# The first unit's third d_ff step in plain blocks: a fused attention and star-ReLU MLP kernel

## Chip, cores and metric

The kernel runs on 1 core of one Trainium2 chip. The metric is the device time of one execution in microseconds; the median of 4 runs of the kernel before is 912.08 us (910.40 to 912.98).

## The reference

Linear attention per head, with a root-mean-square norm, then an MLP on the 4608 tokens (8 batches x 576) of 512 features:

```python
kv = np.einsum('bhsd,bhse->bhde', k, v)
out = np.einsum('bhsd,bhde->bhse', q, kv)
x = out / np.sqrt(np.mean(out * out, axis=-1, keepdims=True) + 1e-06) * g_norm
...
h = x @ w_in            # 512 -> 2048
r = np.maximum(h, 0.0)
g = s * (r * r) + b
return g @ w_out        # 2048 -> 512
```

All is float32 but the two weight matrices, which arrive with 64 bits an element; the kernel makes float32 of them itself.

## The kernel before, in words

**Units and stages.** The tokens are worked in nine units of 512. A unit has a first stage (x @ w_in, and the activation) and a second stage (g @ w_out). The attention of the next unit is laid between the matmuls. The order of instructions on each engine is the order in which the program's Python calls them: the schedule is written out by hand, and an engine takes its instructions in that order.

**First stage.** The 2048 columns of w_in are four steps s = 0 to 3 of 512 columns. A step can be computed in two ways.
- In plain blocks (`mm1_plain`, L671): four blocks of 256 columns x 256 tokens over all 512 features, each 8 matmuls 128x128 by 256. In the order a11, a12, a21, a22 they alternate between the PSUM tiles x and y (two buffers each). ACT takes the x blocks out with a ReLU and DVE squares them (L691); DVE takes the y blocks out with a clamp (L686) and squares them.
- By a scheme of seven products (`mm1`, L707): a Strassen-Winograd step, which forms sums of quarters of w_in and of x first and then needs seven products of 4 matmuls where plain blocks need eight. They are x1, z2, x6, y7, x5, x3, y4. x1, x6, x5 and x3 add up in one PSUM tile x; after x1, x6 and x5 ACT copies the intermediate sum to SBUF (L718) before the next product may add to the tile. `sums_w_in(s)` (L264) makes the sums of w_in on DVE, in two halves: s12 (two operations, of which the second is needed by x6) and s34 (two more: the one for y7, and the one for x3). `x_sums(u)` (L601) makes the four sums of x, in two halves.

The affine pass s * g + b of the activation runs on ACT (L644). In unit 0 it is put off: finished squares go on a list, and `scale_g` (L667) empties it.

**Weights in unit 0.** Sixteen blocks of weights (0 to 7 w_in, two to a step; 8 to 11 the upper half of w_out, `w_up`; 12 to 15 the lower, `w_dn`) are loaded by the SP queue into three buffers `w_raw` (`load_w`, L185). Each is converted in four operations: `raw(i)` is two on ACT (L225, L230), `convert(i)` two on DVE (L235, L245). When a block's conversion is done, the load three blocks ahead is sent (`plus`, L1510). `more(i)` makes a difference of w_out quarters on DVE, in w_up itself.

**The order around the change.** In unit 0, steps 0 and 1 run in plain blocks (the list `slots0`, eight slots, L1536), steps 2 and 3 by the scheme. `first_unit` (L1633) writes the order out: the dictionary `beside` says which conversions, sums and the like are called after each slot's block, and after each slot comes scale_g. Then the products of step 2 (a) and step 3 (b) follow in one list, mixed with conversions 8 to 12. The last two products of step 3, x3 and y4, come after the first product of the second stage (L1786 on), and conversions 13 to 15 lie in the second stage's first slots. There the SP queue also stores sums of w_out to DRAM for the later units (`store_w2`, L315), loads K and V of batch 1 and the q of unit 1.

**Unit 1** runs all four steps by the scheme, so that the sums of w_in that unit 0 did not need must be made there: sums_w_in(0) late in unit 0's second stage, and in `sides` (L1685) sums_w_in(1) at point 1 of step 0 (after z2). Points 2 and 3 follow x6 and y7.

Of the kernel before, what the change touches and what calls it, by code (L numbers as in the profile page):

```python
# [16 lines left out]
def kernel(  # L17
# [53 lines left out]
    NS = FC // 4  # L71
# [192 lines left out]
    def sums_w_in(s):  # L264
        ws[s] = wp.tile([P, 3, KH, 2, P], FP32, name=f"ws_{s}")
        a11, a12 = wa[s][:, :KH], wa[s][:, KH:]
        a21, a22 = wb[s][:, :KH], wb[s][:, KH:]
        s1, s2, s4 = (ws[s][:, i] for i in range(3))

        def s12():  # L270
            add(s1, a21, a22)
            sub(s2, s1, a11)

        def s34():
            sub(a21, a11, a21)
            sub(s4, a12, s2)

        return s12, s34
# [383 lines left out]
    def g_s1(s):  # L662
        add(ga["s1", s], ga["a21", s], ga["a22", s])
# [3 lines left out]
    def scale_g():  # L667
        while to_scale:
            affine(to_scale.pop(0))
# [863 lines left out]
    gp = ctx.enter_context(tc.tile_pool(name="gp", bufs=NS // 2))  # L1533


    slots0 = [slot for s in range(2) for slot in mm1_plain(s)]  # L1536
    turn[0]()
    turn[1]()
    take[0]()
# [85 lines left out]
    def raw(i):  # L1625
        hi(i)
        lo(i)

    def convert(i):
        shift(i)  # L1630
        plus(i)

    def first_unit():  # L1633
        sums = {}

        def of_w(s, k):
            if k == 0:
                sums[s] = sums_w_in(s)
            sums[s][k]()

        of_x = x_sums(0)
        beside = {
            1: [partial(raw, 3), partial(convert, 3)],
            2: [partial(raw, 4), partial(convert, 4)],
            3: [partial(raw, 5), partial(convert, 5)],
            4: [partial(raw, 6), partial(of_w, 2, 0), of_x[0]],
            5: [partial(raw, 7), partial(of_w, 2, 1), partial(g_s1, 0)],
            6: [partial(raw, 8), of_x[1], partial(convert, 6)],
            7: [partial(convert, 7)],
        }  # L1650
        for n, slot in enumerate(slots0):
            if n > 1:
                out_of = slot()
                if out_of:
                    out_of()
            for fn in beside.get(n, []):
                fn()
            scale_g()
        a, b = (mm1(0, s) for s in (2, 3))
        for fn in (  # L1660
            a["x1"], partial(g_s1, 1), partial(of_w, 3, 0),
            a["z2"],
            a["x6"], partial(of_w, 3, 1), partial(raw, 9), scale_g,
            a["y7"], partial(convert, 8),
            a["x5"], partial(raw, 10),
            b["x1"], partial(convert, 9), scale_g,
            a["x3"], partial(more, 8),
            b["z2"], partial(raw, 11),
            a["y4"], a["y4_square"], partial(convert, 10),
            b["x6"], a["x3_s1"], scale_g,  # L1670
            b["y7"], partial(convert, 11),
            b["x5"], partial(raw, 12), partial(more, 9), partial(more, 10), partial(more, 11),
            partial(convert, 12), scale_g,
        ):
            fn()
        return b

    def x3(a):
        a["x3"]()
# [5 lines left out]
    def sides(u, A, B):  # L1685

        first, second = {}, {}
        kv = []  # L1690
        if u in kv_due:
            kv.append(lambda: kv_product(kv_due[u], u > 2))
            kv.append(lambda: used(*((u, "kv", (n, m)) for n in range(NP) for m in range(2))))
        q = {half: [partial(loads, u + 2, half)] for half in range(2)}
        if u == 1:
            first[0, 1] = list(sums_w_in(1))
            first.update({
                (1, 3): kv,
                (2, 0): [partial(A["turn"], 0), partial(A["turn"], 1)],
                (2, 1): [A["product"]],  # L1700
                (2, 2): [A["back"]],
                (2, 3): [A["square"]],
                (3, 0): [A["row_sum"]],
                (3, 2): [A["norm"], A["turn_x"]],
                (3, 3): [lambda: [load() for load in load_q(12, rest_on=nc.sync)]],
            })
            return first, second
        if u + 1 == U:
            return first, second
        if u == 2:  # L1710
            first = {
                4: [A["turn"]],
                5: kv,
                8: [A["product"]],
                9: [A["back"], B["turn"]],
                10: [A["square"]],
                11: [A["row_sum"]],
                12: [B["product"]],
                13: [A["norm"]],
                14: [A["turn_x"]],  # L1720
                15: [B["back"], *q[0]],
            }
            second = {
                0: [B["square"]], 1: [B["row_sum"], A["scale"]], 2: [B["norm"]], 3: [B["turn_x"], *q[1]],
                "sums": [B["scale"]],
            }
        else:
            first = {
                2: [A["turn"]],
                4: [A["product"], *kv],  # L1730
                5: [A["back"]],
                6: [A["square"], B["turn"]],
                7: [A["row_sum"]],
                8: [A["norm"]],
                9: [A["turn_x"]],
                10: [B["product"], *q[0]],
                11: [B["back"], A["scale"]],
                12: [B["square"]],
                13: [B["row_sum"]],
                14: [B["norm"]],  # L1740
                15: [B["turn_x"], *q[1]],
            }
            second = {1: [B["scale"]]}
        second[5], second[6] = [[lambda n=n: x_sums(u + 1)[n]()] for n in range(2)]
        return first, second

    for u in range(U):
        A, B = pairs_of(u + 1) if u + 1 < U else (None, None)
        if u == 0:
            last = first_unit()  # L1750
            second = mm2(0)
        else:
            if u == 1:
                loads(2, 0)
                loads(2, 1)
            first, at_second = sides(u, A, B)
            if u > 1:
                run, last = mm1_deep(u)
                second = mm2(u, last, at_second)
                run(lambda n: [fn() for fn in first.get(n, [])], second["early"])  # L1760
                second["rest"]()
                continue
            steps = [mm1(u, s) for s in range(NS)]
            second = mm2(u)
        for s in range(NS if u > 0 else 0):
            a = steps[s]

            def at(n):
                for fn in first.get((s, n), []):
                    fn()  # L1770

            at(0)
            a["x1"]()
            if s:
                x3(steps[s - 1])
            a["z2"]()
            at(1)
            if s:
                y4(steps[s - 1])
            a["x6"]()  # L1780
            at(2)
            a["y7"]()
            at(3)
            a["x5"]()
        side = side_of(A, B, lambda: [fn() for fn in x_sums(u + 1)], u)
        for n, slot in enumerate(second):  # L1786
            slot()
            if u == 0:
                if n == 0:
                    store_w2(1, 5)  # L1790
                    for name in ("x3", "y4", "y4_square"):
                        last[name]()
                    raw(13)
                    scale_g()
                    convert(13)
                    load_kv(1, 0, convp, tag="raw", bufs=3)
                    raw(14)
                    last["x3_s1"]()
                elif n == 1:
                    convert(14)  # L1800
                    load_kv(1, 1, convp, tag="raw", bufs=3)
                    raw(15)
                    loads(1, 0)
                    loads(1, 1)
                elif n == 2:
                    convert(15)
                    t2 = convp.tile([P, 4 * R * D], FP32, name="w_t2", tag="raw", bufs=3)
                    W2_AT[6] = t2[:, : FC // 2 * HN].rearrange("p (f n) -> p f n", n=HN)
                elif n == 4:
                    store_w2(3, 2)  # L1810
                    sub_w_out(6, 3, 5)
                    store_w2(6)
            if n == 0 and u > 0:
                x3(steps[-1])
                y4(steps[-1])
            for step in side.get(n, []):
                step()
        if u == 0:
            tc_late()
            pump()  # L1820
# [30 lines left out]
```

## Time and profile before

| What | Value |
|---|---|
| median of 4 runs (lowest to highest) | 912.08 us (910.40 to 912.98) |
| the profiled execution's own time | 911.95 us |
| its span, first to last instruction | 910.1 us, so 1.85 us lie around it |
| mean granted clock of TensorE over the span | 0.998 |
| unit 0's first stage: end of the eighth plain block, first product of step 2 | 53.03 us |
| first product of unit 0's second stage | starts 78.58 us |
| w_raw loads sent between 37 and 47 us, from issue to landing | 5.4 to 6.1 us |
| w_raw loads sent between 56 and 80 us | 4.9 to 5.1 us |

Engines are PE (matmul), PEld (its weight load), DVE, ACT, POOL and SP. A row of the timeline gives the start in us from the span's start, the length, the engine, the line of the program, the operation with the tile it writes and those it reads, the shape, how many, and in brackets how long the engine sat idle before it and who ended that. On PE one float32 matmul of 256 columns leaves two records, so x8 is a product of four matmuls and x16 a plain block of eight. Lengths of matmuls overlap with the next one; the time a group takes is read from its start to the start of the next. The chain of waits follows the last instruction of a stretch back, at each step to what released it.

### The profile page before, as it was taken

How to read it: one execution, taken by the hardware profiler on the slowest of the kernel's cores; microseconds unless marked ns; L12 is line 12 of the kernel's file. 1: busy time of each engine (PE TensorE's matmuls, PEld its weight loads, DVE VectorE, ACT ScalarE, POOL GpSimd, SP SyncE). 2: the span in 40 equal slices, each digit the busy share in tenths (PEclk: the TensorE clock that was granted, in tenths of full speed). 3: DMA queues.
4: the chain of work that ended last, by engine and by line, in shares of the span. 5: the costliest groups of instructions: out<-in, count | busy, mean ns of one | idle time of the engine just before them, and what ended most of it. 6: DMA issues, size and time to landing. Idle time of an engine off the chain costs nothing.

```text
span 910.1 us, 19226 instructions
## 1 busy us (share of the span) xinstructions
PE 896.7 (99%) x7506; PEld 824.1 (91%) x7506; DVE 667.7 (73%) x1234; ACT 359.5 (40%) x606; POOL 227.5 (25%) x432
## 2 busy tenths in 40 slices
PE   7989999999999999999999999999999999999998
PEld 6878888888889998999889998999899989999998
DVE  2898676588557985887678857895878778874686
ACT  2878224531147215640366026701580057104710
POOL 2000016113524242810273035603440300021000
PEclk9999999999999999999999999999999999999999
DMA  9657977339943894379636973597438812891286
GB/s 257 220 187 248 286 192 233 104 82 370 354 142 76 276 337 145 78 227 309 215 70 177 294 258 90 123 309 255 132 87 283 293 36 56 275 304 49 58 257 184
DMA packets 120139, 180.34 MB, mean 198 GB/s; under 512 B 29169, under 2 KB 46321, under 8 KB 120049
## 3 DMA queue, kind: packets, MB, share of 16 engines
q1 hardware_dynamic: 101552, 153.00, 54.1%
q0 software_dynamic: 15040, 23.88, 9.1%
q10 hardware_dynamic: 3456, 2.23, 1.0%
q8 instruction: 60, 0.98, 0.5%
q14 instruction: 31, 0.25, 0.1%
HBM read 153.36 MB, written 25.69 MB: 197 GB/s over the span
## 4 chain that ended last, share of the span: by engine, by line
PE 90%; DVE 5%; DMA 2%; ACT 1%; issue 1%; ACTq 0%; DVEq 0%
PE x_ps L91 47%; PE y_ps L91 26%; PE z_ps L91 9%; PE sx_ps L91 4%; PE y_ps L545 2%; DMA kv_sb<-in_v_dram 1%; PE kv_ps L366 1%; PE z_ps L366 1%; DMA w_raw<-in_moe_w_in_dram 1%; DVE xs L253 1%; DVE xn L578 0%; DVE a L253 0%; DVE wa L245 0%; DVE sub L253 0%; PE y_ps L366 0%
## 5 line engine op out<-in xcount | busy, mean ns | idle before, releaser
L1623 POOL DMA_DIRECT2D q_sb<-in_q_dram x256 | 143.6, 569 | 133.9 <-ACT a L652 63.0
L1210 POOL DMA_DIRECT2D out_dram<-o x110 | 54.8, 505 | 399.1 <-issue 152.6
L91 PE MATMUL x_ps<-w_sb,sub 128*128 128x128 f32 x1176 | 148.8, 275 | 0.6 <-DVE r L250 0.6
L91 PEld LDWEIGHTS x_ps<-w_sb,sub 128*128 128x128 f32 x1176 | 139.7, 192 | 0.9 <-DVE r L250 0.9
L91 PE MATMUL x_ps<-xs,ws 128*128 128x256 f32 x544 | 130.0, 382 | 2.9 <-ACT r L718 2.9
L91 PE MATMUL y_ps<-xs,wb 128*128 128x256 f32 x544 | 129.1, 382 | 0.0
L644 ACT ACTIVATE a<-a,b_col,s_col 128x512 f32<-128x512 f32 x144 | 116.2, 813 | 25.5 <-DVE a L647 20.9
L91 PEld LDWEIGHTS x_ps<-xs,ws 128*128 128x128 f32 x544 | 100.3, 191 | 15.9 <-ACT r L718 3.7
L91 PEld LDWEIGHTS y_ps<-xs,wb 128*128 128x128 f32 x544 | 101.4, 191 | 13.6 <-issue 0.6
L819 ACT COPY a<-x_ps 128x512 f32<-128x512 f32 x28 | 16.4, 584 | 216.0 <-PE x_ps L91 215.8
L91 PE MATMUL x_ps<-xT,wa 128*128 128x256 f32 x336 | 78.3, 381 | 0.1
L250 DVE TENSOR_TENSOR r<-sx_ps,a 128x256 f32<-128x256 f32 x63 | 26.6, 422 | 62.1 <-PE sx_ps L91 62.0
L91 PEld LDWEIGHTS x_ps<-xT,wa 128*128 128x128 f32 x336 | 62.2, 190 | 9.7 <-issue 1.5
L91 PE MATMUL x_ps<-w_sb,a 128*128 128x128 f32 (+1 forms) x432 | 64.9, 298 | 0.0
L91 PE MATMUL y_ps<-w_sb,a 128*128 128x128 f32 (+1 forms) x416 | 62.1, 295 | 0.0
L91 PEld LDWEIGHTS x_ps<-w_sb,a 128*128 128x128 f32 x432 | 58.9, 191 | 3.3 <-issue 0.4
L91 PEld LDWEIGHTS y_ps<-w_sb,a 128*128 128x128 f32 x416 | 56.1, 192 | 2.1
L250 DVE TENSOR_TENSOR a<-y_ps,r 128x512 f32<-128x512 f32 x40 | 27.6, 689 | 41.1 <-PE y_ps L91 30.8
L250 DVE TENSOR_TENSOR r<-x_ps,o 128x256 f32<-128x256 f32 (+1 forms) x84 | 29.7, 353 | 29.3 <-PE x_ps L91 28.6
L91 PE MATMUL y_ps<-w_sb,sub 128*128 128x128 f32 x392 | 49.5, 275 | 0.0
L647 DVE SCALAR_TENSOR_TENSOR a<-a 128x512 f32<-128x512 f32 x67 | 46.4, 692 | 2.3
L253 DVE TENSOR_TENSOR a<-a,a 128x512 f32<-128x512 f32 x72 | 46.8, 684 | 0.4
(185 smaller groups left out, 1513.1 us busy)
## 6 DMA issues: line engine op xcount, KB each, us to landing
w_sb<-w SPq DMA_DIRECT2D x385, 256.0 KB, 4.5
w_raw<-in_moe_w_in_dram SPq DMA_DIRECT2D x8, 1024.0 KB, 6.1
w_raw<-in_moe_w_out_dram SPq DMA_DIRECT2D x8, 1024.0 KB, 5.0
w_sb<-w SPq DMA_DIRECT2D x14, 512.0 KB, 8.9
w<-sub POOLq DMA_DIRECT2D x28, 256.0 KB, 6.4
w_sb<-in_k_dram SPq DMA_DIRECT2D x24, 288.0 KB, 5.6
w_sb<-in_v_dram SPq DMA_DIRECT2D x24, 288.0 KB, 5.7
out_dram<-o POOLq DMA_DIRECT2D x92, 64.0 KB, 4.0
```

What stands on the lines that cost most here:

```text
L91: nc.tensor.matmul(o, lhsT=lhsT, rhs=rhs, start=start, stop=stop, skip_group_check=True)
L250: nc.vector.tensor_tensor(out=o, in0=a, in1=b, op=ALU.add)
L253: nc.vector.tensor_tensor(out=o, in0=a, in1=b, op=ALU.subtract)
L366: nc.tensor.matmul(ps[r][(r ^ l) * HB : (r ^ l) * HB + HB, i, :], lhsT=kv[l][0][rows, j, :], rhs=kv[l][1][rows, j, :], start=(j == 0), sto ...
L545: nc.tensor.matmul(ps[l][32 * p : 32 * p + 32, r, lo:hi], lhsT=bd_kv[b % 2][rows, p, at : at + 32], rhs=st["qT"][rows, p, lo:hi], start=Tr ...
L644: nc.scalar.activation(t, t, AF.Identity, scale=s_col, bias=b_col)
L647: nc.vector.scalar_tensor_tensor(t, t, 0.0, t, ALU.max, ALU.mult)
L819: nc.scalar.copy(g_tile("a11", s), st["x", s])
L1210: queues[s % 2].dma_start(out=view[b, jj, :, cols], in_=st[name, j][s * w : s * w + w, cols])
L1623: load()
```

## The change

Unit 0 runs step 2 in plain blocks too: `slots0` has twelve slots, and only step 3 uses the scheme. The order around it is new. After the block of slot n (1 to 8) come raw(n + 2) and convert(n + 2), one conversion to a slot; after slot 9 come the first half of sums_w_in(3) and more(8), after slot 10 the sums of x around raw(11), after slot 11 the second half of sums_w_in(3). g_s1 comes after the blocks of slots 4 and 8, ahead of the conversions. Conversions 11 and 12 lie among the five products of step 3, with raw(13) behind them; convert(13) stays in the second stage's first slot. The sums of w_in for step 2, no longer made in unit 0, are made in unit 1's step 0 at point 3, ahead of x5.

```diff
-    slots0 = [slot for s in range(2) for slot in mm1_plain(s)]
+    slots0 = [slot for s in range(NS - 1) for slot in mm1_plain(s)]
...
     def first_unit():
...
-        beside = {
-            1: [partial(raw, 3), partial(convert, 3)],
-            2: [partial(raw, 4), partial(convert, 4)],
-            3: [partial(raw, 5), partial(convert, 5)],
-            4: [partial(raw, 6), partial(of_w, 2, 0), of_x[0]],
-            5: [partial(raw, 7), partial(of_w, 2, 1), partial(g_s1, 0)],
-            6: [partial(raw, 8), of_x[1], partial(convert, 6)],
-            7: [partial(convert, 7)],
-        }
         for n, slot in enumerate(slots0):
             if n > 1:
                 out_of = slot()
                 if out_of:
                     out_of()
-            for fn in beside.get(n, []):
-                fn()
-            scale_g()
-        a, b = (mm1(0, s) for s in (2, 3))
+                if n % 4 == 0:
+                    g_s1(n // 4 - 1)
+            if 0 < n < 9:
+                raw(n + 2)
+                convert(n + 2)
+            elif n == 0:
+                continue
+            elif n == 9:
+                of_w += sums_w_in(3)
+                of_w[0]()
+            elif n == 10:
+                of_x[0]()
+                raw(11)
+                of_x[1]()
+            else:
+                of_w[1]()
+            if n < 11:
+                scale_g()
+            if n == 9:
+                more(8)
+        a = mm1(0, NS - 1)
         for fn in (
-            a["x1"], partial(g_s1, 1), partial(of_w, 3, 0),
-            a["z2"],
-            a["x6"], partial(of_w, 3, 1), partial(raw, 9), scale_g,
-            a["y7"], partial(convert, 8),
-            a["x5"], partial(raw, 10),
-            b["x1"], partial(convert, 9), scale_g,
-            a["x3"], partial(more, 8),
-            b["z2"], partial(raw, 11),
-            a["y4"], a["y4_square"], partial(convert, 10),
-            b["x6"], a["x3_s1"], scale_g,
-            b["y7"], partial(convert, 11),
-            b["x5"], partial(raw, 12), partial(more, 9), partial(more, 10), partial(more, 11),
-            partial(convert, 12), scale_g,
+            a["x1"], scale_g, partial(convert, 11), partial(more, 9),
+            a["z2"], partial(raw, 12),
+            a["x6"], scale_g, partial(g_s1, 2),
+            a["y7"], partial(convert, 12),
+            a["x5"], partial(raw, 13), scale_g, partial(more, 10), partial(more, 11),
         ):
             fn()
...
         if u == 1:
-            first[0, 1] = list(sums_w_in(1))
+            for s in range(1, NS - 1):
+                first[((0, 1), (0, 3))[s - 1]] = list(sums_w_in(s))
...
                     for name in ("x3", "y4", "y4_square"):
                         last[name]()
-                    raw(13)
+                    convert(13)
                     scale_g()
-                    convert(13)
```

More of the change, by code (lines that the diff above doesn't have):

```diff
@@ L1633, in first_unit @@
     def first_unit():
[L1634 to L1639, printed above, removed]
-        of_x = x_sums(0)
-        beside = {
-            1: [partial(raw, 3), partial(convert, 3)],
-            2: [partial(raw, 4), partial(convert, 4)],
-            3: [partial(raw, 5), partial(convert, 5)],
-            4: [partial(raw, 6), partial(of_w, 2, 0), of_x[0]],
-            5: [partial(raw, 7), partial(of_w, 2, 1), partial(g_s1, 0)],
-            6: [partial(raw, 8), of_x[1], partial(convert, 6)],
-            7: [partial(convert, 7)],
-        }
+        of_x = x_sums(0)
+        of_w = []
         for n, slot in enumerate(slots0):
@@ L1655, in first_unit @@
                     out_of()
-            for fn in beside.get(n, []):
-                fn()
-            scale_g()
-        a, b = (mm1(0, s) for s in (2, 3))
-        for fn in (
-            a["x1"], partial(g_s1, 1), partial(of_w, 3, 0),
-            a["z2"],
-            a["x6"], partial(of_w, 3, 1), partial(raw, 9), scale_g,
-            a["y7"], partial(convert, 8),
-            a["x5"], partial(raw, 10),
-            b["x1"], partial(convert, 9), scale_g,
-            a["x3"], partial(more, 8),
-            b["z2"], partial(raw, 11),
-            a["y4"], a["y4_square"], partial(convert, 10),
-            b["x6"], a["x3_s1"], scale_g,
-            b["y7"], partial(convert, 11),
-            b["x5"], partial(raw, 12), partial(more, 9), partial(more, 10), partial(more, 11),
-            partial(convert, 12), scale_g,
+                if n % 4 == 0:
[19 more added lines that the diff above has]
+        a = mm1(0, NS - 1)
+        for fn in (
+            a["x1"], scale_g, partial(convert, 11), partial(more, 9),
[3 more added lines that the diff above has]
+            a["x5"], partial(raw, 13), scale_g, partial(more, 10), partial(more, 11),
         ):
             fn()
-        return b
+        return a
     def x3(a):
```

## The prediction

> **What bounds the kernel now.** The page first: how full each engine is.
>
> ```profile
> span 910.1 us, 19226 instructions
> ...
> PE 896.7 (99%) x7506; PEld 824.1 (91%) x7506; DVE 667.7 (73%) x1234; ACT 359.5 (40%) x606; POOL 227.5 (25%) x432
> ```
>
> PE is the bound: time is gained only by fewer PE instructions, or by taking away one of PE's rare waits. PE's waits by releaser show that the longest is a single one:
>
> ```profile
> PE x_ps L91 <- ACT r L718: 2.9, 1, 2.9
> ```
>
> The stretches around it (PE, PEld, DVE, ACT and POOL busy, granted clock, DMA share, GB/s):
>
> ```profile
> 53.00:56.50 3.50, 3.50 (x17) 2.86 (x16) 3.47 (x6) 2.81 (x3) 0.00 (x0) 1.00 0.00 0
> 56.50:59.50 3.00, 0.15 (x1) 0.00 (x0) 2.93 (x5) 1.28 (x2) 0.00 (x0) 1.00 0.40 115
> ...
> 60.43:63.85 3.42, 3.42 (x10) 2.72 (x9) 3.35 (x7) 1.37 (x2) 0.00 (x0) 0.50 1.01 338
> ```
>
> While PE stands still DVE is full, and 0.9 us after PE resumes its clock is 0.50 for 3.4 us. The timeline of PE gives the size of both, row by row (start, length):
>
> ```profile
> 53.03 1.89 PE L91 MATMUL x_ps<-xT,wa 128*128 128x256 f32 x8
> 54.76 1.89 PE L91 MATMUL z_ps<-xT,wa 128*128 128x256 f32 x8
> 59.52 2.92 PE L91 MATMUL x_ps<-xs,ws 128*128 128x256 f32 x8 [2.87 <-ACT r L718]
> 62.24 2.69 PE L91 MATMUL y_ps<-xs,wb 128*128 128x256 f32 x8
> 64.76 1.89 PE L91 MATMUL x_ps<-xs,ws 128*128 128x256 f32 x8
> ...
> 78.58 3.62 PE L91 MATMUL x_ps<-w_up,a 128*128 128x256 f32 x16
> ```
>
> The reader is to take starts, not lengths: a product of the scheme (x8 here) takes 1.73 us from start to start, a plain block (x16) 3.45 (49.58 to 53.03). The chain of waits says why x6 of the third step starts late:
>
> ```profile
> 54.95 0.61 DVE wa L235
> 55.57 0.02 issue
> 55.59 1.23 DVE wa L245
> 56.82 0.61 DVE a L686
> 57.43 0.02 issue
> 57.45 0.70 DVE a L691
> 58.16 0.03 issue
> 58.18 0.81 ACT a L644
> 59.00 0.48 ACT r L718
> ```
>
> x1 was done at 54.9, but its copy (L718) stood on ACT behind the affine pass (L644) of the last plain block, and that stood behind DVE, which did sums and a conversion (L235, L245) before it looked at the block (L686, L691). DVE's backlog is the cause.
>
> **The change on PE.** Both kernels are alike up to the end of the eighth plain block at 53.03. From there to the first product of the second stage (78.58) before has 12 products: 12 x 1.727 = 20.72 us. The stretch is 25.55, so 4.83 are lost: 2.87 of waiting, 1.19 and 0.76 in the two products at the half clock (2.92 and 2.48, by starts, against 1.73). After has four plain blocks and five products: 4 x 3.454 + 5 x 1.727 = 22.45 us. So the plain third step costs 1.73 more (13.82 against 12.09), the lost 4.83 go, and without a new wait the second stage starts at 75.48: 3.10 us gained. PE is fed without any longer wait from there on, so a shift passes through to the end.
>
> **What is late next.** I place the new order by the durations of before. On DVE an independent 128x512 operation starts 0.60 us after the last, one that needs the last 0.72 (the rows at 51.26 to 54.87 and 57.45); a conversion takes 0.72 + 1.14 = 1.86. Both kernels' DVE finishes block 5 at 46.66. Until the square of the twelfth block is done, DVE then has five conversions (9.3), four clamp-and-square pairs (5.32), three single squares (1.8), two sums s1 (1.2), two w sums (1.32), one w_out difference (0.6), four x sums (2.52), one square at the head (0.61): 22.7 us, so 69.3. Conversions in before also waited on ACT for 0.21 to 0.56 us in this stage; three at 0.3 make it 70.2. The block itself leaves PE at 66.85, so DVE is some 2 us behind, but what hangs on it has room:
> - x6 (70.31) needs the copy r1, whose ACT is free: done at 69.4. Room 0.9.
> - y7 (72.03) needs the difference in wb, next on DVE: 70.9. Room 1.1.
> - x5 (73.76) needs the copy r2 of x6. On ACT it stands behind the affine pass of the twelfth block (0.72) and raw(12), 1.05 + 1.05 with L225 and L230: 70.3 + 0.72 + 2.1 = 73.15, copy 0.58: 73.75. **Room none.** Each further 0.1 us on DVE is 0.1 us on PE here.
> - The second stage (75.5) needs w_up: converted at 73.4. Room 2.1.
>
> What can make DVE later are the loads: three w_raw buffers, and each load is sent when the conversion three blocks earlier ends. Those sent at 37.6 to 46.8 took 5.4 to 6.1 us beside each other, w_out blocks sent alone 4.9 to 5.1. Now w_out blocks are sent every 3.2 to 3.4 us, two in flight. ACT ends raw(8) at 55.0, as in before, and after one affine pass wants block 9 at 55.7; sent at 50.1, it lands at 55.3 if it takes 5.2 us. With 4.9 the wait at x5 is about 0.1, with 6.1 about 1.0. I take 5.2 to 5.4, nearest to the row at 46.75 (5.37, a w_out load beside another), and **0.3 us**. DMA has room for it: 338 to 419 GB/s in busy stretches, and 1.05 MB every 3.3 us is 318.
>
> **Other edits, at nothing.** x sums, w_out differences and g_s1 are the same operations, moved; they are in the sum above. convert(13) moves into the second stage with more room than before, since w_dn is wanted at 92.8 and the conversions end some 4 us earlier. The SP queue's stores, K/V and q loads come behind the w_raw loads; those end about 7 us earlier, PE's need only 3. The four sums of the third step move to unit 1, 4 x 0.6 = 2.4 us of DVE ahead of a22 of step 0. There DVE is idle 1.55 and then 3.16 us (147.10 and 151.68), and a22, 0.9 late, must be read by 151.4: it covers them. With that cover gone, up to 2.4.
>
> **Sum.** -4.83 + 1.73 + 0.3 = -2.8. The profiled execution took 911.95 (0.13 below the median of 912.08): 909.15, on the median 909.3. I say 909.2.
>
> **A rule against it.** The half clock is 1.95 of the 4.83 and goes only if the wait caused it. The row: 2.87 us idle, then 0.50 for 3.4 us. The Trainium skill, "TensorE: Matmul & The Clock Gate", Part 1, "What's actually happening", says the clock halves after at least one idle window of about 3.4 us, windows running free. By that rule 2.87 us isn't enough, the half clock had another cause and stays, and the sum is -0.85. The trace decides here: its half clock lasts one such stretch, directly after the only long wait.
>
> **Rivals.**
> - *Late loads* (10%): the new pace makes loads take 6.5 to 7 us; block after block reaches ACT late, x6, y7 and x5 wait 1.2 to 2.0 us in all. 911.95 - 3.10 + 1.2 to 2.0 = 910.05 to 910.85. For it: the DMA share is 1.01 in busy stretches, and the first three w_raw loads, sent together, took 7.6 to 11.6. Against: those three landed 2.7 us apart, faster than the new pace.
> - *The half clock stays* (6%): it began after PE had resumed, so another cause isn't excluded. 909.15 + 1.95 = 911.1.
> - *Unit 1 doesn't hide the moved sums* (5%): up to 909.15 + 2.4 = 911.55. Against: the 4.7 us of idle DVE.
> - *Slower* (8%): the wait comes back one step later. With loads at 8 to 9 us (three abreast took that), x6 of the fourth step waits 1.3 to 2.3, with y7 and x5 3.0 to 4.0 in all, and the clock halves again (1.95): 911.95 + 1.73 - 4.83 + 5.0 to 6.0 = 913.8 to 914.8. It decides from 3.1 us of loss on, a halved clock included.
> - *Forecast* (71%): wait 0 to 0.9, so 908.85 to 909.75.
>
> **How the numbers follow.** This measurement tells about 0.2%, 1.8 us, from no change: faster means below 910.26. The forecast and about 3 of the late loads' 10 are there: 0.74. The rest of the late loads, the half clock and unit 1 lie within: 0.18. Slower 0.08. The range goes from 908.3 (no wait, less half a us by which medians of such runs differ: 910.4 to 912.98 are seen) to 911.2, which takes in late loads and the half clock.
>
> **What would show it.** Right: PE's wait of 2.9 us on r L718 is gone, the clock is 1.00 from 53 to 80, the third step is four rows of x16 at 53.0, 56.5, 59.9, 63.4, the second stage starts at 75.5 to 75.9, and x5 there waits below half a us for r L718. Wrong: a clock of 0.50 again, idle time ahead of x6 or y7 released by DVE xs, wb or ACT r, w_raw loads above 6.5 us, or a new wait of PE in unit 1, step 0 or 1.

## Result and profile after

The kernel after takes 911.02 us (median of 44 runs, 909.27 to 912.48); the kernel before, beside it, 912.02 (63 runs, 909.67 to 914.01). The ratio is 0.9989, 95% interval 0.9984 to 0.9993: 1.0 us gained where 2.8 were forecast, which is within the 0.2% that count as no change. The profiled execution of after took 911.34 (span 909.6), that of before 911.95.

PE's waits by releaser in the kernel after, from 15 to 140 us; the columns are total, times, longest:

```profile
PE x_ps L91 <- ACT r L718: 1.1, 2, 0.8
...
PE y_ps L91 <- DVE wb L253: 0.5, 1, 0.5
```

The one wait of 2.9 us is gone, and three small ones have come. PE's timeline of the kernel after has them in place:

```profile
53.18 3.62 PE L91 MATMUL x_ps<-xT,wa 128*128 128x256 f32 x16
56.63 3.62 PE L91 MATMUL y_ps<-xT,wb 128*128 128x256 f32 x16
...
66.99 1.89 PE L91 MATMUL x_ps<-xT,wa 128*128 128x256 f32 x8
68.72 1.89 PE L91 MATMUL z_ps<-xT,wa 128*128 128x256 f32 x8
70.89 1.99 PE L91 MATMUL x_ps<-xs,ws 128*128 128x256 f32 x8 [0.28 <-ACT r L718]
73.39 1.97 PE L91 MATMUL y_ps<-xs,wb 128*128 128x256 f32 x8 [0.51 <-DVE wb L253]
76.14 1.99 PE L91 MATMUL x_ps<-xs,ws 128*128 128x256 f32 x8 [0.79 <-ACT r L718]
77.97 2.32 PE L91 MATMUL x_ps<-w_up,a 128*128 128x256 f32 x10
```

Take starts again. The four plain blocks take 3.45 us each, 53.18 to 66.99. The five products take 10.98 where 5 x 1.727 = 8.64 were due: 2.34 lost. The brackets add up to only 1.58: the product ahead of a wait is counted to its end (1.89, 1.99 and 1.97 long), 0.16 to 0.26 past the 1.73 at which the next could have started, and the last product took 1.83 from start to start. The second stage begins at 77.97; before, it was 78.58. The 0.61 is the whole gain of the profiled pair: -4.83 + 1.73 + 2.34, and 0.15 because the first eight blocks ended later (53.18 against 53.03).

The same stretch of the windows that stood at a clock of 0.50 before (PE, PEld, DVE, ACT and POOL busy, granted clock, DMA share, GB/s), in the kernel after:

```profile
60.43:63.85 3.42, 3.42 (x18) 3.01 (x17) 3.19 (x5) 3.42 (x5) 0.00 (x0) 1.00 0.96 323
```

The clock is full, and ACT, not DVE, is busy all the time. What ended last ahead of x5 (the row at 76.14) is in the chain of waits from 66 to 78 us of the kernel after:

```profile
69.41 1.90 DVE xs L253 x3
71.31 0.61 DVE a L686
71.92 0.02 issue
71.94 0.70 DVE a L691
...
73.39 1.16 ACT w_raw L225
74.55 1.07 ACT w_raw L230
75.62 0.47 ACT r L718
```

This is the chain that the prediction worked out, square, affine pass, raw(12), copy, but DVE comes to the square 2.4 us later than it said. The reason is thirty microseconds earlier, in the loads. From issue to landing, the load of block 6 (issued at 40.39 before, at 39.68 after), first the kernel before, then the kernel after:

```profile
w_raw<-in_moe_w_in_dram SPq DMA_DIRECT2D x1, 1024.0 KB, 5.9
```

```profile
w_raw<-in_moe_w_in_dram SPq DMA_DIRECT2D x1, 1024.0 KB, 8.0
```

Sent 0.7 us sooner, it lands at 47.63 in place of 46.28. The loads of blocks 5 to 9:

| Block | before: sent, took (us) | after: sent, took (us) |
|---|---|---|
| 5 | 37.55, 5.61 | 37.70, 6.17 |
| 6 | 40.39, 5.89 | 39.68, 7.95 |
| 7 | 43.38, 6.12 | 43.33, 7.61 |
| 8 | 46.75, 5.37 | 47.45, 7.44 |
| 9 | 56.88, 4.94 | 51.20, 6.41 |

Why block 6 is sent sooner is a line of the diff that the prediction passed over. Before, scale_g came after every slot, slot 0 too; after, `elif n == 0: continue` leaves it out. So the first two affine passes no longer stand ahead of raw(3) on ACT, conversion 3 ends 0.7 us earlier, and the load that it releases follows the one before after 2.0 us in place of 2.8. ACT in the kernel after:

```profile
35.63 1.18 ACT L225 ACTIVATE w_raw<-w_raw 128x1024 f32<-128x1024 f32 x1
36.67 1.19 ACT L230 ACTIVATE w_raw<-w_raw 128x1024 uint32<-128x1024 uint32 x1
37.74 1.53 ACT L644 ACTIVATE a<-a,b_col,s_col 128x512 f32<-128x512 f32 x2
...
43.96 1.16 ACT L225 ACTIVATE w_raw<-w_raw 128x1024 f32<-128x1024 f32 x1 [1.42 <-DMA w_raw<-in_moe_w_in_dram]
```

Before, the pair of L644 ran at 35.50, ahead of raw(3) at 36.91. After block 5's wait (1.42; 0.84 before), ACT waits for DMA three times more, 0.36, 0.41 and 0.55, once for each of the next three blocks.

### The profile page after: what moved, and what is told of

Read it like the earlier page. It is cut to its first block, busy times and chain, and to the rows that moved or that the text cites. A ratio compares the mean times of both kernels' runs of the same rounds, so it can differ in the third digit from the quotient of the medians.

```text
span 909.6 us, 19247 instructions
## 1 busy us (share of the span) xinstructions
PE 897.6 (99%) x7514; PEld 824.7 (91%) x7514; DVE 667.4 (73%) x1234; ACT 358.0 (39%) x603; POOL 228.3 (25%) x432
## 4 chain that ended last, share of the span: by engine, by line
PE 88%; DVE 6%; DMA 4%; ACT 1%; issue 1%; DVEq 0%; ACTq 0%
PE x_ps L91 46%; PE y_ps L91 25%; PE z_ps L91 9%; PE sx_ps L91 4%; PE y_ps L545 2%; DMA w_raw<-in_moe_w_in_dram 2%; DMA q_sb<-in_q_dram 1%; DMA w_raw<-in_moe_w_out_dram 1%; PE kv_ps L366 1%; PE z_ps L366 1%; DVE xs L253 1%; DMA kv_sb<-in_k_dram 1%; ACT w_raw L230 0%; DVE xn L578 0%; DVE a L253 0%
## 5 line engine op out<-in xcount | busy, mean ns | idle before, releaser
L644 ACT ACTIVATE a<-a,b_col,s_col 128x512 f32<-128x512 f32 x144 | 116.3, 813 | 30.7 <-DVE a L647 24.2
L91 PE MATMUL x_ps<-xs,ws 128*128 128x256 f32 x528 | 125.4, 380 | 1.1 <-ACT r L718 1.1
L91 PE MATMUL y_ps<-xs,wb 128*128 128x256 f32 x528 | 124.6, 381 | 0.5 <-DVE wb L253 0.5
L91 PEld LDWEIGHTS y_ps<-xs,wb 128*128 128x128 f32 x528 | 97.5, 190 | 13.6 <-PE x_ps L91 0.9
L91 PEld LDWEIGHTS x_ps<-xs,ws 128*128 128x128 f32 x528 | 96.7, 190 | 13.9 <-ACT r L718 2.3
L91 PE MATMUL x_ps<-xT,wa 128*128 128x256 f32 x360 | 83.7, 381 | 0.1
L91 PEld LDWEIGHTS x_ps<-xT,wa 128*128 128x128 f32 x360 | 66.8, 190 | 10.3 <-issue 1.5
L91 PE MATMUL z_ps<-w_sb,a 128*128 128x128 f32 (+1 forms) x352 | 46.8, 280 | 0.0
```

Source lines behind the costliest of these rows:

```text
L91: nc.tensor.matmul(o, lhsT=lhsT, rhs=rhs, start=start, stop=stop, skip_group_check=True)
L644: nc.scalar.activation(t, t, AF.Identity, scale=s_col, bias=b_col)
```

## Experiments

Theory: the spacing of the loads made them late, late blocks made DVE late, and DVE made PE wait at x6, y7 and x5. Rivals: the order of ACT or DVE makes PE wait whatever the loads do; five products cannot be fed at all behind twelve plain blocks. Chips differ a little (before had medians of 911.4 to 912.1), so ratios are compared; each is to the runs of before beside it.

### Hiding the loads: two more buffers (a_five_buffers)

```diff
-        dst = convp.tile([P, 4 * R * D], U32, name="w_raw", tag="raw", bufs=3)
+        at = sent[0] % 5 - 3 if sent[0] < 10 else -1
+        if at >= 0:
+            dst = w_dn.rearrange("p f n -> p (f n)")[:, at * 4 * DM : at * 4 * DM + 4 * DM].bitcast(U32)
...
-    for _ in range(3):
+    for _ in range(5):
         send_w()
```

> The kernel after, with five buffers for the weight loads in place of three: the two more lie in w_dn, whose place is free until block 12 is converted. Five loads are sent at the start and each later one when the conversion five blocks before it ends; nothing is left out. Loads theory (three buffers and loads of 6 to 8 us make ACT and DVE late): the waits ahead of x6, y7 and x5 of step 3 (0.3, 0.5 and 0.8 us) go, the second stage starts at about 75.6 in place of 78.0, and the time falls by some 2.2 us, 0.25% below after and about 3 us below before. Order theory (the order on DVE and ACT makes them late, whatever the loads take): the waits stay, the same time as after within 0.5 us.

Measured: 908.71 us (908.5 to 909.17, 7 runs), ratio 0.9972 (0.9961 to 0.9984). PE doesn't wait from 33 to 100 us, and 52.93 to 75.37 is 22.44, the 22.45 of the prediction. The loads sent from 37 us on still take up to 7.4 us, and neither ACT nor DVE waits for one. So the five products can be fed, and the price of the plain step was right.

### Only what stands ahead of x6's copy (a_raw12_late)

```diff
-            a["z2"], partial(raw, 12),
-            a["x6"], scale_g, partial(g_s1, 2),
+            a["z2"],
+            a["x6"], partial(raw, 12), scale_g, partial(g_s1, 2),
```

> The kernel after, with raw(12) behind x6 and its copy on ACT in place of ahead of it. Loads theory: only the wait ahead of x5 shrinks (0.8 to about 0.1), those ahead of x6 and y7 stay; 0.5 to 0.7 us faster than after. Order theory: with the one misplaced conversion gone nearly all of the 2.3 us of waits goes. Both: w_raw loads sent from 37 to 55 us again take 6 to 8 us if that belongs to the new pace; 5.4 to 6.1 if what the trace of after shows was a slow moment of that run.

Measured: 909.79 (908.93 to 910.9, 11 runs), 0.9979 (0.9970 to 0.9988). Block 6 is again sent 2.0 us behind block 5 and takes 8.27, the next two 7.31 and 7.24, but only y7 waits (0.39); 22.45 us of work take 23.07 (52.79 to 75.86), 0.62 lost. So late loads cost less when raw(12) doesn't stand between the affine pass and the copy: they needed that order to reach x5.

### The dropped affine call put back (a_affine_first)

```diff
             elif n == 0:
+                scale_g()
                 continue
```

> The kernel after, with the affine passes of the first two blocks on ACT ahead of raw(3), as in before; so the second of the sustained loads (block 6) is sent about 2.8 us behind the first again, in place of 2.0. Spacing theory (the loads of 7 to 8 us come from sending these two close together): they return to 5.6 to 6.1 us, and the time falls by 1 to 1.5 us against after. Pace theory (a load every 3.3 us keeps the DMA engines nearly full, whatever the start): loads from 43 us on again take 6.5 to 8 us; the same time as after within 0.7 us.

Measured: 909.22 (908.83 to 911.0, 11 runs), 0.9977 (0.9968 to 0.9986). Block 6 is sent 2.83 us behind block 5 and takes 6.01; blocks 7 to 10 take 6.27, 5.24, 4.91 and 4.89. PE waits once, 0.23 at x5; the second stage starts at 76.02. One line brings the time close to the forecast: 909.2 of 912.08 is a ratio of 0.9968, at the edge of this interval.

### The kernel after once more (after_again)

> The kernel after unchanged, beside the others on one chip. Pace theory: its runs spread by 2 to 3 us, as the loads of each run make the conversions more or less late, about a median 1 us below before. If the wide spread was that of several chips, the runs lie within 1 us here.

Measured: 910.29 (909.95 to 913.27, 11 runs), 0.9990 (0.9980 to 1.0000). Block 6 took 8.08:

```profile
70.82 1.89 PE L91 MATMUL x_ps<-xs,ws 128*128 128x256 f32 x8
72.72 1.97 PE L91 MATMUL y_ps<-xs,wb 128*128 128x256 f32 x8
75.45 1.99 PE L91 MATMUL x_ps<-xs,ws 128*128 128x256 f32 x8 [0.76 <-ACT r L718]
77.28 3.62 PE L91 MATMUL x_ps<-w_up,a 128*128 128x256 f32 x16
```

It repeats the ratio, the slow load and the wait at x5, but not every wait: x6 starts on time and y7 0.17 late, and 53.55 to 77.28 are 23.73, 1.28 lost in place of 2.34. Blocks 7 to 9 took 7.09, 6.62 and 5.03 here. The runs spread over 3.3 us on this one chip, so the spread isn't that of several chips.

### Which load: block 7 held back (a_load7_later)

The affine call moves both ACT and the loads. Two kernels keep after's order on ACT, DVE and PE and hold back one load: an addition on POOL, into a tile that nobody reads, must read the buffer first.

```diff
     def plus(n, h=None):
+        src = w_raw[blocks[n]].bitcast(FP32)[:, : 2 * TB]
         add_lo(blocks[n], place(n), h)
+        if n == 4:
+            t = rp.tile([P, 2, TB], FP32, name="later", tag="ra").rearrange("p a b -> p (a b)")
+            nc.gpsimd.tensor_tensor(out=t, in0=src, in1=place(n)[:, : 2 * TB], op=ALU.add)
         if h != 0:
             send_w()
```

> The kernel after, its order on ACT, DVE and PE unchanged; one addition on POOL reads the w_raw buffer of block 4 and its place after the conversion, into a tile that nobody reads, so that the load of block 7 is sent later (39.7 to 40.0 us before, by about 0.7 to 1.2 us). Theory (the spacing of the loads): the loads sent after it take 5.8 to 6.4 us in place of 7 to 8, PE waits ahead of x6, y7 and x5 together at most 0.5 us, second stage from about 76.2 or earlier, time 909.0 to 909.7. Rival (the affine passes' own place on ACT costs the time, and the loads only go with it): load times of 7 us or more stay, or the waits of 0.3 and 0.8 us stay although the loads are short, time 910.2 to 911.0. POOL's addition may itself cost DVE some tenths.

Measured: 911.53 (909.8 to 912.63, 11 runs), 0.9992 (0.9983 to 1.0001): no better than after. The send that the expectation names, at 39.7 to 40.0, is block 6's; the edit held back block 7, which after sends at 43.33, 0.5 us before block 5 lands. So it tells whether that third load in flight is the cause. Sent at 44.36, 0.7 us after block 5 had landed, block 7 did take 6.09; but the load of block 6 had already been slow, with only one other in flight for most of its time:

```profile
w_raw<-in_moe_w_in_dram SPq DMA_DIRECT2D x1, 1024.0 KB, 8.1
```

It landed at 47.49, and PE still waited 0.24 at y7 and 0.75 at x5. A third load in flight is not the cause.

### Which load: block 6 held back (a_load6_later)

The same with `if n == 3` and 320 columns.

> The kernel after, its order on ACT, DVE and PE unchanged; an addition of 128x320 on POOL reads the w_raw buffer of block 3 and its place after the conversion, into a tile that nobody reads, so that the load of block 6 is sent about 0.8 to 1.0 us later, some 2.8 us behind that of block 5 in place of 2.0, as in the kernel before. Theory now (the gap between the loads of blocks 5 and 6 decides): block 6's load takes 5.8 to 6.4 us in place of 8 and lands earlier than without the delay (by 47.0 us), blocks 7 and 8 take 6.5 us at most, PE's waits ahead of x6, y7 and x5 are 0.5 us or less together, time 909.0 to 909.8. Rival (a third load in flight, or the place of the affine passes on ACT, not the gap): block 6's load still lands at 47.3 us or later, the waits stay near 1.0 to 1.6 us, time 910.2 to 911.5.

Measured: 909.42 (908.77 to 909.54, 6 runs), 0.9968 (0.9956 to 0.9980). POOL's addition and the load of block 6 behind it:

```profile
39.47 0.88 POOL L1515 TENSOR_TENSOR later<-w_raw,wb 128x320 f32<-128x320 f32 x1 [28.32 <-DVE wb L245]
```

```profile
w_raw<-in_moe_w_in_dram SPq DMA_DIRECT2D x1, 1024.0 KB, 6.2
```

The send of block 5 has no record in this trace; by the end of conversion 2 the gap is about 2.9. Sent at 40.38 in place of 39.68, it lands at 46.63 in place of 47.63: **later sent, sooner there**. Blocks 7 to 9 take 6.15, 5.09 and 5.01, and PE is left with one wait:

```profile
71.91 1.89 PE L91 MATMUL y_ps<-xs,wb 128*128 128x256 f32 x8
74.28 1.99 PE L91 MATMUL x_ps<-xs,ws 128*128 128x256 f32 x8 [0.48 <-ACT r L718]
```

So the gap between the loads of blocks 5 and 6 decides here, not the affine passes' own place and not a third load. In the three-buffer traces in which both sends show, a gap of 2.0 us gave 7.95, 8.08, 8.13 and 8.27, one of 2.8 gave 5.89, 5.95 and 6.01. Where the gap has to be taken from the end of conversion 2, 2.8 gave 5.87 in a_affine_raw12, but 6.89 in b_reordered (below). With five buffers the pair is blocks 7 and 8: 7.10 and 7.43 at 2.0, 6.46 and 6.92 at 2.8. The direction holds everywhere; the size doesn't.

### Both small edits (a_affine_raw12)

scale_g at slot 0 and raw(12) behind x6, three buffers.

> The kernel after with both small edits: scale_g at slot 0 (the first two affine passes ahead of raw(3), as in the kernel before) and raw(12) behind x6. Three buffers. Theory: the loads are spaced (5.2 to 6.4 us), the last copy of x6 no longer stands behind raw(12), so no wait above 0.15 us is left between 53 and 76; second stage at 75.5 to 75.8, time 908.7 to 909.1, level with the five buffers (908.71) without their second set of loads. Rival (the five buffers gain elsewhere, in the second stage): 909.2 or more, as with the affine passes alone.

Measured: 908.98 (908.68 to 910.78, 8 runs), 0.9973 (0.9963 to 0.9983). PE has no wait from 40 to 140 us:

```profile
71.84 1.89 PE L91 MATMUL y_ps<-xs,wb 128*128 128x256 f32 x8
73.57 1.89 PE L91 MATMUL x_ps<-xs,ws 128*128 128x256 f32 x8
75.30 3.62 PE L91 MATMUL x_ps<-w_up,a 128*128 128x256 f32 x16
```

From 52.85 to 75.30 are 22.45 us. With these two small edits, the changed kernel gives what five buffers give.

### What a wait of 2.5 us does to the clock (a_five_gap)

Five buffers and raw(12) behind x6, so that PE would not wait, and six needless copies on ACT that make it wait at x6:

```diff
             keep("r1", st["x"], "ra")
+            if u == 0:
+                for _ in range(6):
+                    keep("r1", st["x"], "rb")
```

> The kernel after with five load buffers and raw(12) behind x6, and a wait made on purpose: six more copies of x1's PSUM tile stand on ACT ahead of the copy that x6 waits for, so that PE idles about 2.7 us at 70 us. Nothing is left out. If such a wait halves the clock for 3.4 us (as in the trace of before): 908.7 + 2.7 + 1.7 = 913.1 in the runs in which it does, 911.4 in those in which it does not, so two groups 1.7 us apart. If a wait of that length never does it and the half clock of before had another cause: all runs near 911.4.

Measured: 912.71 (911.0 to 913.61, 11 runs), 1.0012 (1.0001 to 1.0023). The profiled execution (911.82) waited and kept its clock, as the row and the window behind it show:

```profile
73.17 1.99 PE L91 MATMUL x_ps<-xs,ws 128*128 128x256 f32 x8 [2.53 <-ACT r L721]
```

```profile
73.20:76.60 3.40, 3.40 (x16) 3.01 (x17) 2.49 (x4) 1.97 (x3) 0.00 (x0) 1.00 0.69 200
```

But the runs fall into two groups: five at 911.0 to 911.82 with a mean granted clock of 0.999 to 1.000, six at 912.71 to 913.61 with 0.997 or 0.998. All 7 runs of a_five_buffers, without the wait, stand at 0.999 or 1.000. The kernel before falls into groups too. Its 83 runs beside the experiments, by their mean granted clock:

| Mean granted clock | runs of before | median (lowest to highest), us |
|---|---|---|
| 1.000 | 28 | 910.21 (909.72 to 910.85) |
| 0.998 | 43 | 912.01 (911.31 to 912.78) |
| 0.996 | 12 | 913.37 (912.99 to 914.42) |

The groups don't overlap. A stretch of 3.4 us at half clock is 0.19% of the span, one step of the table, and costs 1.7 us of matmul. So by their mean clock about two runs of three of before have a half clock, and six of eleven here; the same wait can leave the clock whole. Traces of the halved runs of a_five_gap, and of those of before at 0.996, which lost a second step, are not kept. All 44 runs of after stand at 0.999 or 1.000.

### The other way: the scheme kept, the order mended

Could the kernel before be mended without plain blocks? First only the affine pass that blocked x1's copy, moved behind it (b_copy_first):

```diff
-            scale_g()
+            if n < 7:
+                scale_g()
...
-            a["x1"], partial(g_s1, 1), partial(of_w, 3, 0),
+            a["x1"], scale_g, partial(g_s1, 1), partial(of_w, 3, 0),
```

> The kernel before, with the last affine pass of the plain blocks moved on ACT behind the copy of x1 of step 2. If the place of that copy on ACT alone were the cause of the wait of 2.9 us: about 4.8 us faster than before (the half clock goes too), 907.2. Loads theory: DVE's backlog remains, so a wait of 2.5 to 3 us comes back some products later (ahead of x3 of step 2, or x6 of step 3), and the time is between before less 2 and before. Whether the clock is halved after a wait of about 2.5 us is seen too.

Measured: 909.19 (908.87 to 909.51, 9 runs), 0.9980 (0.9970 to 0.9989). x6 doesn't wait; 1.74 us of wait come back at x3 of the third step, and the second stage starts at 75.56. Then the same with five buffers (b_copy_first_five):

> The kernel before (steps 2 and 3 by the scheme) with both edits: the copy of x1 ahead of the affine pass, and five buffers for the weight loads. Loads theory: no wait of PE from 33 to 110 us, the second stage starts at about 73.8 in place of 78.6, no half clock; some 4.8 us faster than before, 907.2, and faster than the kernel after with five buffers by the 1.73 us that a plain step costs more than one by the scheme. Order theory: DVE's other work (sums and conversions) holds PE up by 2 to 3 us all the same, 909.5 to 911.

Measured: 908.14 (907.93 to 909.01, 5 runs), 0.9967 (0.9954 to 0.9979), so the 907.2 without a wait didn't come. The wait at x3 is 1.00, with blocks there in time: DVE, back to back, comes late to z2's sum, the affine pass waits for it on ACT, and the copy that x3 needs stands behind. So the scheme's last microsecond is an order on DVE and ACT, not a load. With that order mended too (b_reordered_five), z2's sum ahead of the sums for the fourth step and raw(11) behind its x6:

```diff
-            a["x1"], partial(g_s1, 1), partial(of_w, 3, 0),
-            a["z2"],
+            a["x1"], scale_g,
+            a["z2"], partial(g_s1, 1), partial(of_w, 3, 0),
...
-            b["z2"], partial(raw, 11),
+            b["z2"],
...
-            b["x6"], a["x3_s1"], scale_g,
+            b["x6"], partial(raw, 11), a["x3_s1"], scale_g,
```

> The kernel before (steps 2 and 3 by the scheme), with five load buffers, the copy of x1 ahead of the last affine pass, z2's sum ahead of the sums of step 3 on DVE, and raw(11) behind x6 of step 3 on ACT. Expected if only the order and the loads stood in the way of the scheme: one wait of about 0.5 us ahead of x5 of step 3, second stage at about 74.5 to 75, 907.7 in all, 1 us below the kernel after with five buffers and 0.5 below the variant with one edit less. If DVE's work for two scheme steps simply doesn't fit: the waits of 1 us move on and the time stays at 908.1 or above.

Measured: 908.04 (907.87 to 908.84, 5 runs), 0.9963 (0.9950 to 0.9976), the lowest here. One wait is left, 0.35 at the last x5; the second stage starts at 74.78. And with three buffers (b_reordered):

> The kernel before with its order changed (last affine pass behind x1's copy, z2's sum ahead of the sums for step 3, raw(11) behind x6 of step 3), both steps by the scheme, three buffers. With five buffers the same order took 908.04. If the buffers count for the scheme too: waits ahead of x3 of step 2 or in step 3 return (0.5 to 1.5 us), second stage at 75.3 to 76.3, 908.6 to 909.5. If only the order counts: second stage at 74.2 to 75.0 (the first loads are not crowded), 907.4 to 908.2, the fastest of all.

Measured: 909.79 (908.58 to 911.38, 12 runs), 0.9980 (0.9971 to 0.9990), nearer to the dearer branch and beyond it. PE, and ACT ahead of the copy that it waits for:

```profile
66.02 1.99 PE L91 MATMUL x_ps<-xT,ws 128*128 128x256 f32 x8 [2.20 <-ACT r L718]
```

```profile
62.62 1.16 ACT L225 ACTIVATE w_raw<-w_raw 128x1024 f32<-128x1024 f32 x1 [2.85 <-DMA w_raw<-in_moe_w_out_dram]
```

Block 9 is sent at 57.18, when conversion 6 ends, and lands at 62.53: with three buffers the scheme has to wait for it. So in this order the scheme needs the buffers too, while the plain step of after does without. The intervals of b_reordered_five and a_affine_raw12 (0.9950 to 0.9976, and 0.9963 to 0.9983) overlap.

## Why the prediction was right in its mechanism and wrong in its size

The time lies inside the stated range, but near its upper end, in the part that was there for the rivals. The likeliest answer ("faster", 0.74) and the forecast's own 908.85 to 909.75 (71%) both missed.

1. **PE's count: right.** "4 x 3.454 + 5 x 1.727 = 22.45", measured 22.44 and 22.45 in the kernels without waits. The plain step costs 1.73 more.
2. **The wait of 2.87 and the half clock go: right.** All runs of after have the full clock. But the half clock was counted as if each run of before paid it. Of 83 runs 28 don't. Beside after_again, on one chip, the 12 such runs have a median of 910.18, and after has 910.29: what after gains there is the half clock, and no more. The starts agree, if those runs waited as long as the traced one: 3.04 of waiting gone, against 1.73 for the plain step and 1.28 lost in after_again, leaves 0.03. The profiled execution was of the middle kind, near the median, so the sum against it stands, but the step took a chance for a certainty. Its split of the 4.83 also misread the rows: 2.92 is a length and 2.48 stands in no row; by starts the two products took 2.72 and 2.52, so the half clock cost 1.79, not 1.95, and the wait 3.04. The sum of 4.83 is right all the same.
3. **"I take 5.2 to 5.4 ... and 0.3 us": this step failed.** The loads of blocks 6 to 9 took 6.4 to 8.0, and the waits cost 2.34 by starts (1.28 in after_again) in place of 0.3. Nor was "the new pace" of w_out loads, which the rival of late loads named, the cause: at the same pace, a_affine_first had 4.9 to 5.5 us for them. One earlier load, block 6, started it, and the blocks behind inherited the delay. The forecast rested on "Both kernels' DVE finishes block 5 at 46.66", where after's finished at 47.4: it took the stretch ahead of 53 us for unchanged, though the diff drops a call there. PE was unchanged there, ACT's order wasn't.
4. **"Room none" at x5: right to a tenth.** DVE's twelfth square ended at 72.64 where 70.2 was forecast, 2.4 late; x5 started at 76.14 in place of 73.76, 2.4 late. (Its 73.15 adds up to 73.12; nothing rests on that.)
5. **Late loads as a rival: right in place, too small.** It named x6, y7 and x5 and 1.2 to 2.0 us, for 6.5 to 7 us a load; the result is just above its 910.85.
6. **The moved sums in unit 1: right.** PE doesn't wait from 100 to 200 us in either kernel.
7. **The rule on the clock: the trace was rightly preferred, but both were too firm.** The Trainium skill, "TensorE: Matmul & The Clock Gate", Part 1, asks for at least one idle window of about 3.4 us. The runs contradict that length: the trace of before has a half clock after a wait of 2.87 us, and six of the eleven runs of a_five_gap, whose traced wait is 2.53, have the mean clock of one. That page also says the windows run free; a wait that halves the clock in one run and not in the next would fit that, though no run here shows the windows.

The sum, rewritten with what was measured: -4.83 + 1.73 + 2.34 + 0.15 = -0.61 for the profiled pair, -1.0 for the medians. Part of after's own spread of 3 us, at a full clock, is in these waits (2.34 and 1.28 in its two traces, with the loads behind block 6 slower in the first); the rest stays open.

## What to carry to other kernels

When a diff rewrites an order, list each engine's calls one by one against the old order, from the first line that differs and not from where PE differs; a call that is dropped, an affine pass of 1.5 us here, can move a load, and a load sent sooner can land later. Look for the instruction with no room (the copy behind raw(12)) and move it or what stands ahead of it: here that made the same late loads cost about 1 us less (0.9979 against 0.9989 and 0.9990; the intervals overlap a little, and by starts the loss was 0.62 against 2.34 and 1.28). A half clock seen in one profile is a chance: look at the mean granted clock of every run before putting its whole price into a sum.

## What the runs showed of the hardware

- **Two loads of 1 MB close together.** A load sent 2.0 us behind another took 7.95 to 8.27 us, one sent 2.8 behind mostly 5.87 to 6.01, and landed about a microsecond earlier. A gap of about 2.9 gave 6.25 (a_load6_later), one of 2.8 also 6.89 (b_reordered), and with five buffers the two gaps gave 7.10 and 7.43 against 6.46 and 6.92. The one ahead of it took 5.6 to 6.3 either way. Why the closer pair moves less (341 GB/s against 368, from 40.4 to 43.0 us) stays open; gaps in between were not tried.
- **The clock and short waits.** A single wait of 2.2 us (b_reordered; 3 of 12 runs at 0.998), 2.53 (6 of 11) or 2.87 (55 of 83) went with a half clock in part of the runs only, by their mean clock; a wait of 1.74 (b_copy_first) in none of 9. Each wait is that of the kernel's one traced run; only before's trace shows the half clock itself.
- **POOL beside DVE.** While POOL's addition ran (39.47 to 40.35), a square on DVE that began at 39.50 took 1.39 us in place of 0.69; beside the longer addition (43.05 to 44.33) one begun at 43.60 took 1.27. Both ended 0.54 us after POOL did. The Trainium skill, "SBUF — State Buffer", "Terms", says the two share a port pair that one of them holds for a whole instruction; these rows agree, though 0.54 is less than the 0.69 that a whole square takes, which stays open.
